# Attention and expert layer on one core: pooled exponentials cross through DRAM in 6 transfers a pair instead of 12, with all orders written anew

## The chip, the cores and the metric

The kernel runs on one core of a Trainium2 chip. The metric is the time of one execution on the device in microseconds; the median of three runs counts. A core has a matmul engine (PE, with its weight loads, PEld), a vector engine (DVE), a scalar engine (ACT), GpSimd (POOL) and SyncE (SP), which here only issues DMAs. Each engine works off its own list of instructions in order and waits on semaphores for the others.

## The reference

```python
B, H, S, D = 8, 8, 576, 64; factor = 4; Sd = 144
q_d, k_d, v_d = (mean of q, k, v over groups of 4 positions)      # (B, H, 144, 64)
out_d = softmax(q_d @ k_d.T / 8) @ v_d                            # pooled attention
out_up = np.repeat(out_d, 4, axis=2)
mask = np.abs(pos[:, None] - pos[None, :]) < 4
out_local = softmax(where(mask, q @ k.T / 8, -1e9)) @ v           # local attention
x = (out_up + out_local) as (B * S, H * D) = (4608, 512)
h = x @ w_in                                                      # (4608, 2048)
P = a0 + a1*h + a2*h**2 + a3*h**3
Q = 1 + |b0|*|h| + |b1|*h**2
out = (P / (Q + 1e-6)) @ w_out                                    # (4608, 512)
```

All of it is float32.

## The kernel before

The attention is done in pairs of heads (`Pair`, `slots`), two pairs at a time; I call two such pairs a quad. A batch has two quads. The expert layer runs over nine blocks of 512 tokens, 16 steps of 128 hidden features each, 144 steps in all: the matmuls of L1084 make h, ACT and DVE turn it into g (L1097 to L1190), and the matmuls of L1214 multiply g by w_out. Both products are split in three terms of a shorter float format, so each step has 12 + 12 matmuls of 128x512. From about 40 us on the attention of later batches is worked in between the steps of earlier ones.

The changed code is that of the pooled attention in batches 3 to 7 (`PT_FROM = 3`), ten quads with 20 "far" pairs. There the exponentials `ep` (queries on partitions, 3 groups of 144 keys) must come to lie with the keys on partitions. For that DVE transposes them in blocks of 32 x 32 (`tp`, L751 and L754), SP writes the blocks to DRAM (`bounce_p<-tp`) and reads them back in another order (`eq<-bounce_p`), all in `moved` (L744). The 144 keys are five blocks of 32, the last of which overlaps its neighbour by 16; only its second half is written. So a pair takes 4 writes of 4 blocks, 4 writes of the half block, 2 big and 2 small reads. `far_pooled_v` (L926) then multiplies `eq` by the pooled values `vq`, 48 keys at a time in 3 steps. The exponentials of the local attention take the same way through `tt`, `bounce` and `eu` (4 writes, 2 reads).

The order of everything is found by a planner (`Plan.run`). Each task has an engine, a cost and, for DMAs, a time to landing; it is due as late as its successors allow, moved by a number from the table `SHIFT`, and at each point the ready task that is due first is taken. The lists of all five engines are then issued in that order. The planner's costs of the transfers are `PT_LOADS` and `DT_LOADS`. SP has at most eight transfers open: the ninth waits for the first (`RING`). Where the plan leaves PE idle in the first 40 us, `warm` puts filler matmuls (L1422).

Of the kernel before, what the change touches and what calls it, by code (L numbers as in the profile page):

```python
# [207 lines left out]
def attention_moe(  # L208
# [117 lines left out]
    bounce_p = nc.dram_tensor("bounce_p", [NPAIR * (B - PT_FROM), SD, 2, 5 * BL], F32, kind="Internal").ap()  # L326
# [222 lines left out]
    def q0(c, i):  # L549
        return min(i * D, SD - D) if far_pooled(c) else i * QC  # L550
# [181 lines left out]
    def turned_blocks(cs, bk, due):  # L732
# [13 lines left out]
        for c in cs:  # L746
            s = c.slot
            if far_pooled(c):

                def turn(s=s):  # L750
                    nc.vector.transpose(  # L751
                        out=s.tp.ap[:, :4], in_=s.ep.ap[:, :, : 4 * BL].rearrange("p i (b x) -> p b i x", x=BL)
                    )
# [5 lines left out]
                for a in range(4):
                    lo, n = a * BL, 2 + a % 2  # L760
                    for i, src, k, m in (
                        (0, s.tp.ap[lo : lo + BL, :4, :n], 0, 4 * BL), (1, s.tp.ap[lo + BL // 2 : lo + BL, 4:, :n], 4 * BL, BL // 2)
                    ):
                        to = far[k : k + m, a // 2, a % 2 * D : a % 2 * D + n * BL]
                        moved(
                            to.rearrange("(b i) x -> i b x", i=min(m, BL)), src.rearrange("p b i x -> p b (i x)"),
                            (s.tp,), (rooms[i][a],), PT_LOADS[i],
                        )
# [9 lines left out]
            if c.far:  # L778
# [7 lines left out]
                for r in range(2):  # L786
# [88 lines left out]
    def weighted(cs, bk, due):  # L875
# [45 lines left out]
        def far_pooled_v():  # L921
            for k in range(NKC):
                for c, x in zip(cs, ava):
                    for j in range(2):
# [803 lines left out]
```

## Time and profile before

| | |
|---|---|
| median of 3 runs | 953.27 us (951.35 to 953.3) |
| the profiled execution | 953.53 us, its span 951.5 us |
| PE busy | 931.4 us (98%) |
| DVE busy | 874.3 us (92%) |
| ACT busy | 775.4 us (81%) |
| mean granted clock of PE | 0.997 |
| reads `eq<-bounce_p` | 40 of 72 KB, 4.4 us to landing (median); 40 of 9 KB, 2.0 us |
| writes `bounce_p<-tp` | 160 of 4 to 48 KB, 1.9 to 2.4 us |
| loads `qk<-in_qk_dram` | 32 of 590 KB, 6.3 us |

The span runs from the first to the last instruction of the program in the profile; the execution's time has 2.0 us more around it. "Busy" of PE counts modelled ends of overlapping matmuls: one of 128x512 is shown with 0.39 us, and the next starts 0.23 us after it.

### The profile page before, as it was taken

How to read it: one execution, taken by the hardware profiler on the slowest of the kernel's cores; microseconds unless marked ns; L12 is line 12 of the kernel's file. 1: busy time of each engine (PE TensorE's matmuls, PEld its weight loads, DVE VectorE, ACT ScalarE, POOL GpSimd, SP SyncE). 2: the span in 40 equal slices, each digit the busy share in tenths (PEclk: the TensorE clock that was granted, in tenths of full speed). 3: DMA queues.
4: the chain of work that ended last, by engine and by line, in shares of the span. 5: the costliest groups of instructions: out<-in, count | busy, mean ns of one | idle time of the engine just before them, and what ended most of it. 6: DMA issues, size and time to landing. Idle time of an engine off the chain costs nothing.

```text
span 951.5 us, 19814 instructions
## 1 busy us (share of the span) xinstructions
PE 931.4 (98%) x7037; PEld 731.9 (77%) x7037; DVE 874.3 (92%) x1567; ACT 775.4 (81%) x1972; POOL 149.2 (16%) x176
## 2 busy tenths in 40 slices
PE   8999999999999999999989999999999999999996
PEld 7756566777787877787878878787878788887885
DVE  6999999999999999999979999999999888988886
ACT  4899999897897979797969798888979676767664
POOL 1032232221203121222213030404020000000000
PEclk9999999999999999999999999999999999999999
DMA  9697855545355556565646565655633010001001
GB/s 296 253 270 211 253 102 96 147 83 146 53 155 118 123 116 139 147 126 116 124 127 114 140 108 164 116 133 107 170 74 82 5 45 1 1 0 45 1 1 44
DMA packets 97578, 108.24 MB, mean 114 GB/s; under 512 B 29480, under 2 KB 79784, under 8 KB 97480
## 3 DMA queue, kind: packets, MB, share of 16 engines
q1 hardware_dynamic: 73960, 85.80, 30.2%
q0 software_dynamic: 23232, 20.66, 16.2%
q8 instruction: 55, 0.90, 0.4%
q10 hardware_dynamic: 288, 0.52, 0.2%
q14 instruction: 43, 0.35, 0.1%
HBM read 85.95 MB, written 20.99 MB: 112 GB/s over the span
## 4 chain that ended last, share of the span: by engine, by line
PE 47%; DVE 26%; ACT 16%; issue 5%; DMA 3%; SPq 2%; DVEq 0%; ACTq 0%
PE psum L1214 19%; PE psum L1084 17%; ACT m L1097 7%; DVE g L1176 6%; PE psum L1072 4%; DVE m L1181 3%; DVE m L1190 3%; DVE m L1141 3%; DVE m L1146 3%; ACT gb L1097 3%; ACT el L624 2%; PE psum L888 2%; DMA eq<-bounce_p 2%; DVE m L1150 2%; SPq L744 1%
## 5 line engine op out<-in xcount | busy, mean ns | idle before, releaser
L1214 PE MATMUL psum<-wh,g 128*128 128x512 f32 x1152 | 373.1, 398 | 3.2 <-DVE g L1176 2.2
L1214 PEld LDWEIGHTS psum<-wh,g 128*128 128x128 f32 x1152 | 214.9, 188 | 58.2 <-DVE g L1176 5.3
L1084 PE MATMUL psum<-xs,wh 128*128 128x512 f32 (+1 forms) x1040 | 258.1, 388 | 0.8 <-ACT gb L1097 0.8
L1097 ACT ACTIVATE m<-psum,cf 128x512 f32<-128x512 f32 x288 | 213.2, 748 | 26.4 <-PE psum L1084 20.3
L1176 DVE TENSOR_TENSOR g<-m,m 128x512 fp32r<-128x512 f32 x288 | 194.3, 685 | 42.7 <-ACT m L1097 36.4
L1084 PEld LDWEIGHTS psum<-xs,wh 128*128 128x128 f32 x1040 | 192.2, 188 | 42.9 <-ACT gb L1097 2.0
L1214 PE MATMUL psum<-wl,g 128*128 128x512 f32 x576 | 224.5, 391 | 0.0
L1097 ACT ACTIVATE gb<-m 128x512 f32<-128x512 f32 x144 | 93.1, 648 | 65.9 <-DVE m L1141 57.8
L1084 PE MATMUL psum<-xs,wl 128*128 128x512 f32 (+1 forms) x520 | 138.2, 388 | 0.0
L1097 ACT ACTIVATE gb<-psum,cf 128x512 f32<-128x512 f32 x144 | 115.4, 802 | 21.2 <-PE psum L1214 20.7
L1214 PEld LDWEIGHTS psum<-wl,g 128*128 128x128 f32 x576 | 108.4, 188 | 21.5
L1084 PEld LDWEIGHTS psum<-xs,wl 128*128 128x128 f32 x520 | 96.3, 188 | 20.0 <-DVE wl L397 0.3
L1141 DVE SCALAR_TENSOR_TENSOR m<-m,cf,m 128x512 f32<-128x512 f32 x144 | 106.9, 742 | 2.1 <-ACT m L1097 1.1
L441 POOL DMA_DIRECT2D vq<-in_vq_dram x60 | 52.2, 918 | 321.7 <-DMA vq<-in_vq_dram 230.0
L1097 ACT ACTIVATE m<-gb 128x512 f32<-128x512 f32 x144 | 92.7, 647 | 11.6 <-DVE m L1146 9.9
L1181 DVE SCALAR_TENSOR_TENSOR m<-m,g 128x512 f32<-128x512 f32 x144 | 98.8, 686 | 2.3
L441 POOL DMA_DIRECT2D pq<-in_qkp_dram x84 | 73.6, 923 | 170.7 <-DMA pq<-in_qkp_dram 106.9
L1190 DVE TENSOR_TENSOR m<-m,m 128x512 f32<-128x512 f32 x144 | 98.5, 684 | 1.6
L1146 DVE TENSOR_TENSOR m<-m,m 128x512 f32<-128x512 f32 x144 | 98.4, 684 | 1.7 <-ACT m L1097 1.7
L1150 DVE TENSOR_TENSOR m<-m,gb 128x512 f32<-128x512 f32 x144 | 98.2, 682 | 1.8 <-ACT gb L1097 0.4
L1097 ACT ACTIVATE m<-psum 128x512 f32<-128x512 f32 x144 | 87.3, 608 | 0.3
L624 ACT ACTIVATE el<-el,nm 128x64 f32<-128x64 f32 x240 | 80.8, 355 | 1.7 <-DVE nm L616 1.7
(101 smaller groups left out, 903.2 us busy)
## 6 DMA issues: line engine op xcount, KB each, us to landing
qk<-in_qk_dram SPq DMA_DIRECT2D x32, 590.0 KB, 6.3
pq<-in_qkp_dram POOLq DMA_DIRECT2D x84, 144.0 KB, 3.5
vw<-in_vw_dram SPq DMA_DIRECT2D x32, 320.0 KB, 11.5
out_dram<-xf SPq DMA_DIRECT2D x34, 256.0 KB, 2.5
bounce<-tt SPq DMA_DIRECT2D x96, 80.0 KB, 1.9
eu<-bounce SPq DMA_DIRECT2D x40, 160.0 KB, 3.3
sl<-in_w_out_dram SPq DMA_DIRECT2D x12, 512.0 KB, 4.8
vq<-in_vq_dram POOLq DMA_DIRECT2D x60, 96.0 KB, 3.4
```

Of the source, the lines that this page charges most:

```text
L441: lambda d=dst, x=src, r=r: nc.gpsimd.dma_start(out=d.ap, in_=rows(x, r), accum_op=ALU.add),
L624: nc.scalar.activation(out=s.el.ap[:, k, j, :], in_=view[:, j, k, :], func=AF.Exp, bias=nm[:, 5 * j + k : 5 * j + k + 1], scale=scale, acc ...
L1072: nc.tensor.matmul(ph.ap, lhsT=bits[0][fc].ap[:, c, :].bitcast(F32), rhs=x.ap[:, c, :], start=(c == 0), stop=(c == NCC - 1),)
L1084: nc.tensor.matmul(ph.ap[:, f * t : (f + 1) * t], lhsT=(high, low)[j][0][fc].ap[:, c, :], rhs=blk.x[i].ap[:, c, t0 : t0 + t], start=(part_ ...
L1097: add("ACT", cost, lambda: nc.scalar.activation(out=out_.ap, in_=in_, func=func, **kw), (room_in, cf, *more), (out_,))
L1141: lambda: v.scalar_tensor_tensor(out=tb.ap, in0=tq.ap, scalar=b1, in1=tb.ap, op0=ALU.mult, op1=ALU.add),
L1146: add("DVE", 0.602, lambda: v.tensor_tensor(out=ta.ap, in0=ta.ap, in1=tq.ap, op=ALU.mult), (ta, tq), (ta,))
L1150: add("DVE", 0.602, lambda: v.tensor_tensor(out=ta.ap, in0=ta.ap, in1=u.ap, op=ALU.add), (ta, u), (ta,))
L1176: return v.tensor_tensor(out=out, in0=x, in1=y, op=ALU.mult)
L1181: lambda: v.scalar_tensor_tensor(out=tb.ap, in0=tb.ap, scalar=CONE, in1=gh.ap.bitcast(F32), op0=ALU.add, op1=ALU.mult),
L1190: add("DVE", 0.602, lambda: v.tensor_tensor(out=ta.ap, in0=ta.ap, in1=tb.ap, op=op), (ta, tb), (ta,))
L1214: nc.tensor.matmul(ob[sub].ap, lhsT=g[i].ap[:, g0 : g0 + P], rhs=flat((high, low)[j][1][fc].ap), start=(fc == 0 and m == 0), stop=(fc == N ...
```

## The change

Five blocks of 32 keys are taken at a stride of 28 (`KB = 28, NKB = 5`: keys 0 to 31, 28 to 59, ..., 112 to 143), so 160 rows hold the 144 keys, some twice. One DVE transpose makes all five. A pair then takes 4 writes, each of all five blocks, and 2 reads of 64 rows x 3 steps x 144 queries. The matmul contracts over 64 rows instead of 48; the values `vq` have zero rows where a key comes for a second time. The planner's costs of the reads and of the local reads are set anew, and the whole table `SHIFT` is replaced, with which all lists change their order. (Lines after the first are one further down, so L744 is now L745 and L926 is L927.)

```diff
-    bounce_p = nc.dram_tensor("bounce_p", [NPAIR * (B - PT_FROM), SD, 2, 5 * BL], F32, kind="Internal").ap()
+    bounce_p = nc.dram_tensor("bounce_p", [NPAIR * (B - PT_FROM), NKB * BL, 2, SD], F32, kind="Internal").ap()
...
     def q0(c, i):
-        return min(i * D, SD - D) if far_pooled(c) else i * QC
+        return (0, D, SD - QC)[i] if far_pooled(c) else i * QC
...
-                def turn(s=s):
-                    nc.vector.transpose(
-                        out=s.tp.ap[:, :4], in_=s.ep.ap[:, :, : 4 * BL].rearrange("p i (b x) -> p b i x", x=BL)
+                flat_ep = s.ep.ap.rearrange("p i k -> p (i k)")
+                src = bass.AP(
+                    tensor=flat_ep.tensor, offset=flat_ep.offset,
+                    ap=[flat_ep.ap[0], [KB, NKB], [SD, NQ], [1, BL]],
+                )
+                add(
+                    "DVE", 0.57, lambda s=s, src=src: nc.vector.transpose(out=s.tp.ap, in_=src), (s.ep,), (s.tp,)
+                )
+                far = bounce_p[c.p - PT_FROM * NPAIR]
+                rooms = [Room(None, [("E", c.p, a)]) for a in range(4)]
+                for a in range(4):
+                    lo, n = a * BL, D + a % 2 * (SD - 2 * D)
+                    to = far[:, a // 2, a % 2 * D : a % 2 * D + n]
+                    moved(
+                        to.rearrange("(b i) x -> i b x", i=BL), s.tp.ap[lo : lo + BL].rearrange("p b i x -> p b (i x)")[:, :, :n],
+                        (s.tp,), (rooms[a],), PT_LOADS[0],
                     )
-                    nc.vector.transpose(out=s.tp.ap[:, 4], in_=s.ep.ap[:, :, SD - BL :])
-
-                add("DVE", 0.62, turn, (s.ep,), (s.tp,))
...
                 for r in range(2):
-                    own = s.eq.ap[r * D : r * D + KQ]
-                    from_ = [rooms[i][a] for i in range(2) for a in (2 * r, 2 * r + 1)]
-                    moved(own[:, :, : 2 * D], back[r][:, :, : 2 * D], from_, (c.halves[r],), PT_LOADS[2], 0.78)
-                    moved(own[:, :, 2 * D :], back[r][:, :, 2 * D + BL // 2 :], from_[1::2], (c.halves[2 + r],), PT_LOADS[1], 0.78)
+                    row = far[0, r]
+                    back = bass.AP(
+                        tensor=row.tensor, offset=row.offset, ap=[[2 * SD, D], [KQ * 2 * SD, NKC], [1, SD]]
+                    )
+                    moved(
+                        s.eq.ap[r * D : (r + 1) * D], back, rooms[2 * r : 2 * r + 2], (c.halves[r],), PT_LOADS[1], 0.6,
+                    )
...
-                            lhsT=c.vp.ap[m : m + KQ, k, :], rhs=c.slot.eq.ap[m : m + KQ, k, :],
+                            lhsT=c.vp.ap[m : m + D, k, :], rhs=c.slot.eq.ap[m : m + D, k, :],
...
-DT_LOADS = (0.25, 0.8)
+DT_LOADS = (0.25, 1.8)
...
-PT_LOADS = (0.15, 0.1, 0.15)
+PT_LOADS = (0.2, 0.7)
...
 SHIFT = {
-    "alone.0": {0: 4.2, 1: -3.7, 2: -24.3, 3: 193.8},
+    "alone.0": {0: -49.2, 1: -66.5, 2: -2.4, 3: 72.7, 4: -11.7},
...
+    rows = [[KB * (r // BL) + r % BL for r in range(k * KQ, k * KQ + D)] for k in range(NKC)]
     vq = np.zeros((B - PT_FROM, NPAIR, 2, D, NKC, POOL, D), v.dtype)
-    vq[:, :, :, :KQ] = v[PT_FROM:].reshape(B - PT_FROM, NPAIR, 2, NKC, KQ, POOL, D).transpose(0, 1, 2, 4, 3, 5, 6)
+    keys, seen = v.reshape(B, NPAIR, 2, SD, POOL, D), set()
+    for k in range(NKC):
+        for r, key in enumerate(rows[k]):
+            if key not in seen:
+                vq[:, :, :, r, k] = keys[PT_FROM:, :, :, key]
+                seen.add(key)
```

The far quads are numbered 0 to 9 in the order in which PE uses them. On SP, at the end of the second pair of quad 4, before: `tp0` and `eq0` are that pair's pooled exponentials, `eu0` its local ones, `out_0_dram` is an output store, `qk0` the load of q and k for a later pair.

```order
L744 DMA bounce_p<-tp0_201 16x96
L1247 DMA out_0_dram<-xf0_0_154 128x512 x2
L744 DMA bounce_p<-tp0_201 32x4x96
L744 DMA eu0_198<-bounce 64x2x320
L744 DMA bounce_p<-tp0_201 16x96
L744 DMA eu0_198<-bounce 64x2x320
L1247 DMA out_0_dram<-xf0_0_154 128x512
L744 DMA eq0_200<-bounce_p 48x3x16 x2
L423 DMA qk0_191<-in_qk_dram 128x1180
L744 DMA eq0_200<-bounce_p 48x3x128 x2
```

The same place now, from the pair's first write on.

```order
L745 DMA bounce_p<-tp0_201 32x5x80 x2
L745 DMA bounce_p<-tp0_201 32x5x64
L745 DMA bounce<-tt0_193 32x4x160
L1248 DMA out_0_dram<-xf0_0_154 128x512 x2
L745 DMA bounce<-tt0_193 32x4x160
L745 DMA eq0_200<-bounce_p 64x3x144
L1248 DMA out_0_dram<-xf0_0_154 128x512 x2
L745 DMA bounce_p<-tp0_201 32x5x64
L745 DMA eu0_198<-bounce 64x2x320 x2
L745 DMA eq0_200<-bounce_p 64x3x144
L424 DMA qk0_191<-in_qk_dram 128x1180
```

The load `qk0`, which stood ahead of the two big reads, now stands behind the last read.

On SP, at the end of the second pair of quad 3, before:

```order
L744 DMA eq0_200<-bounce_p 48x3x16
L744 DMA bounce_p<-tp0_201 32x4x96
L744 DMA eu0_198<-bounce 64x2x320
L744 DMA bounce_p<-tp0_201 16x64
L744 DMA bounce_p<-tp0_201 16x96
L744 DMA bounce_p<-tp0_201 16x64
L744 DMA eu0_198<-bounce 64x2x320
L744 DMA eq0_200<-bounce_p 48x3x128
L744 DMA eq0_200<-bounce_p 48x3x16
L744 DMA eq0_200<-bounce_p 48x3x128
L423 DMA qk0_191<-in_qk_dram 128x1180
```

And now, where `eu1` and `qk1` belong to the other pair of the quad's slots:

```order
L745 DMA bounce<-tt0_193 32x4x160 x2
L745 DMA eu1_209<-bounce 64x2x320
L745 DMA bounce<-tt0_193 32x4x160
L424 DMA qk1_202<-in_qk_dram 128x1180
L745 DMA bounce<-tt0_193 32x4x160
L745 DMA bounce_p<-tp0_201 32x5x64
L745 DMA bounce_p<-tp0_201 32x5x80 x2
L745 DMA eu0_198<-bounce 64x2x320 x2
L424 DMA qk0_191<-in_qk_dram 128x1180
L745 DMA eq0_200<-bounce_p 64x3x144 x2
```

Here the load `qk0`, which stood behind the reads, now stands ahead of both.

On DVE, around the second pair's transposes in quad 4, before:

```order
L1150 TENSOR_TENSOR m1_162<-m1_162,gb1_172 128x512
L689 TENSOR_TENSOR el0_196<-el0_196,sm0_185 128x640
L751 STREAM_TRANSPOSE tp0_201<-ep0_199 128x384
L754 STREAM_TRANSPOSE tp0_201<-ep0_199 128x96
L776 STREAM_TRANSPOSE tt0_193<-el0_196 128x640
L1176 TENSOR_TENSOR g1_168<-m1_162,m5_166 128x512
```

And now:

```order
L690 TENSOR_TENSOR el0_196<-el0_196,sm0_185 128x640
L1151 TENSOR_TENSOR m1_162<-m1_162,gb1_172 128x512
L777 STREAM_TRANSPOSE tt0_193<-el0_196 128x640
L757 STREAM_TRANSPOSE tp0_201<-ep0_199 128x480
L1177 TENSOR_TENSOR g1_168<-m1_162,m5_166 128x512
L1182 SCALAR_TENSOR_TENSOR m3_164<-m3_164,g1_168 128x512
```

The local transpose `tt0` has changed places with the pooled one.

## Rows read from the trace of the kernel before

**Rows 1.** Page: span, then busy us (share of the span) and instructions
```profile
span 951.5 us, 19814 instructions
...
PE 931.4 (98%) x7037; PEld 731.9 (77%) x7037; DVE 874.3 (92%) x1567; ACT 775.4 (81%) x1972; POOL 149.2 (16%) x176
```

**Rows 2.** Busy us (xinstructions) of PE, PEld, DVE, ACT, POOL by stage; clock; DMA
```profile
48.00:168.00 120.00, 117.94 (x892) 75.02 (x891) 119.61 (x230) 118.72 (x340) 37.22 (x42) 1.00 0.73 187
168.00:744.00 576.00, 569.35 (x4555) 458.43 (x4554) 544.56 (x996) 483.47 (x1292) 109.50 (x126) 1.00 0.54 120
744.00:920.00 176.00, 175.04 (x799) 143.87 (x798) 150.47 (x233) 124.93 (x204) 0.00 (x0) 1.00 0.03 13
```

**Rows 3.** Who waited for whom on PE: us in total, times, longest
```profile
PE psum L926 <- DMA eq<-bounce_p: 5.4, 4, 2.9
```

**Rows 4.** Timeline of PE, quad 4: start, us, instruction [idle before]
```profile
491.09 1.54 PE L926 MATMUL psum<-eq,vq 48*64 48x144 f32 x22 [2.88 <-DMA eq<-bounce_p]
...
494.08 0.79 PE L1214 MATMUL psum<-wh,g 128*128 128x512 f32 x1
...
495.38 0.39 PE L1214 MATMUL psum<-wl,g 128*128 128x512 f32 x1
```

**Rows 5.** The clock beside it: stretch, length, PE busy, granted clock, DMA, GB/s
```profile
491.79:495.20 3.41, 3.41 (x69) 0.50 0.21 58
```

**Rows 6.** Timeline of PE, quad 2
```profile
389.00 1.22 PE L926 MATMUL psum<-eq,vq 48*64 48x144 f32 x22 [0.33 <-DMA eq<-bounce_p]
...
390.97 0.50 PE L1214 MATMUL psum<-wh,g 128*128 128x512 f32 x1
...
391.78 0.39 PE L1214 MATMUL psum<-wl,g 128*128 128x512 f32 x1
```

**Rows 7.** Timeline of DVE, second pair of quad 4
```profile
473.43 0.23 DVE L754 STREAM_TRANSPOSE tp<-ep 128x96 f32<-128x96 f32 x1
```

**Rows 8.** Timeline of the DMA queue of SP, quad 4: issue start, us
```profile
473.54 0.78 SPq L744 DMA_DIRECT2D bounce_p<-tp  x2
...
484.65 0.43 SPq L423 DMA_DIRECT2D qk<-in_qk_dram  x1
...
485.12 0.90 SPq L744 DMA_DIRECT2D eq<-bounce_p  x2
```

**Rows 9.** Timeline of DVE, second pair of quad 3
```profile
424.78 0.23 DVE L754 STREAM_TRANSPOSE tp<-ep 128x96 f32<-128x96 f32 x1
```

**Rows 10.** Timeline of the DMA queue of SP, quad 3
```profile
433.84 1.27 SPq L744 DMA_DIRECT2D eq<-bounce_p  x3
435.16 0.44 SPq L423 DMA_DIRECT2D qk<-in_qk_dram  x1
```

**Rows 11.** Timeline of PE, quad 3
```profile
435.49 1.07 PE L1084 MATMUL psum<-xs,wh 128*128 128x512 f32 x4
436.49 1.32 PE L926 MATMUL psum<-eq,vq 48*64 48x144 f32 x22
```

**Rows 12.** Timeline of DVE, second pair of quad 9
```profile
726.56 0.23 DVE L754 STREAM_TRANSPOSE tp<-ep 128x96 f32<-128x96 f32 x1
```

**Rows 13.** Timeline of PE, quad 9
```profile
738.63 1.41 PE L926 MATMUL psum<-eq,vq 48*64 48x144 f32 x22 [0.69 <-DMA eq<-bounce_p]
```

**Rows 14.** Groups of PE by form: busy us, mean ns | idle before
```profile
L560 PE MATMUL psum<-pq 64*64 64x144 f32 x384 | 17.5, 291 | 0.2 <-DVE el L597 0.2
...
L926 PE MATMUL psum<-eq,vq 48*64 48x144 f32 x240 | 12.9, 299 | 5.4 <-DMA eq<-bounce_p 5.4
```

**Rows 15.** Groups of DVE by form: busy us, mean ns | idle before
```profile
L776 DVE STREAM_TRANSPOSE tt<-el 128x640 f32<-128x640 f32 x24 | 19.9, 830 | 0.0
...
L751 DVE STREAM_TRANSPOSE tp<-ep 128x384 f32<-128x384 f32 x20 | 11.2, 558 | 0.0
...
L754 DVE STREAM_TRANSPOSE tp<-ep 128x96 f32<-128x96 f32 x20 | 4.7, 235 | 0.0
```

More of the change, by code (lines that the diff above doesn't have):

```diff
@@ L29 @@
 NKC, KQ = 3, SD // 3
+KB, NKB = 28, 5
 QR = D + QC
@@ L410, in __init__ @@
             self.vp = (vqs if self.far else vps)[p % 2]
-            self.halves = [Room(None, [("Q", p, i)]) for i in range(6)]
+            self.halves = [Room(None, [("Q", p, i)]) for i in range(4)]
         def pos(self, j):
@@ L748, in turned_blocks @@
             if far_pooled(c):
-                def turn(s=s):
-                    nc.vector.transpose(
-                        out=s.tp.ap[:, :4], in_=s.ep.ap[:, :, : 4 * BL].rearrange("p i (b x) -> p b i x", x=BL)
-                    )
-                    nc.vector.transpose(out=s.tp.ap[:, 4], in_=s.ep.ap[:, :, SD - BL :])
-                add("DVE", 0.62, turn, (s.ep,), (s.tp,))
-                far = bounce_p[c.p - PT_FROM * NPAIR]
-                rooms = [[Room(None, [("E", c.p, a, i)]) for a in range(4)] for i in range(2)]
@@ L759, in turned_blocks @@
[L759 to L768, printed above, removed]
@@ L793, in turned_blocks @@
                     own = s.eu.ap[r * D : (r + 1) * D].rearrange("p (g a) k q -> p g (a k q)", g=2)
-                    moved(own, back, rooms[0] + rooms[1], (c.halves[4 + r],), DT_LOADS[1] / 2, 0.8)
+                    moved(own, back, rooms[0] + rooms[1], (c.halves[2 + r],), DT_LOADS[1] / 2, 0.6)
                 continue
@@ L1528 @@
+    "h.1": {0: -20.3, 2: 19.8, 3: -7.8},
+    "h.2": {0: 24.7, 1: 18, 3: 11.1},
+    "h.3": {0: -13.5, 1: 75.8, 2: 143.6, 3: 129.8},
+    "h.4": {0: 358.8, 1: 33, 2: -21.5, 3: 40.2},
+    "h.5": {0: 15.4, 1: 60.8, 2: 233.8},
+    "h.6": {0: 178.7, 2: 1.1},
+    "h.7": {0: 29.1, 2: 24.2},
     "load": {
-        0: -109.3, 1: -1.8, 2: 1.2, 4: 24.9, 5: -47.2, 6: 18.7, 7: -38.8, 8: 9, 9: -30.9, 10: 1.4,
-        11: -16.5, 12: 23.6, 13: 18.5,
+        0: 39.4, 1: 25.5, 3: -62.4, 4: -7.5, 5: -95.3, 6: 77.7, 7: -169.5, 8: 49.5, 9: 10.3, 10: -2.1,
+        12: -0.1, 13: 20.6,
@@ L1553 @@
-    "middle.1": {
-        0: 99.4, 1: -3.9, 2: -21.5, 3: 15.2, 4: 8.1, 6: 2.6, 7: 41.1, 8: -12.7, 9: 7.8, 10: -2.9, 12: 9.2,
+        1: 19.8, 2: -14.2, 4: 347, 5: 16.7, 6: 1.5, 7: 1, 8: -805, 9: -68.6, 10: 5.3, 11: 5.2, 12: 2.9,
+    },
+    "middle.1": {0: -6.6, 2: 1.8, 4: -113.9, 5: 87.2, 6: -62, 7: -15.5, 8: 29.4, 11: 0.2, 12: 91.1},
+    "middle.2": {
+        0: -1.7, 1: 1.9, 2: 126.7, 3: 24.9, 4: -16.3, 5: 1.2, 6: 0.9, 7: 3.2, 8: -136.2, 9: -42.8, 10: -0.7,
+        11: -5.5, 12: -46.4,
@@ L1555 @@
     },
-    "middle.2": {0: -33.4, 1: 103.1, 2: 1, 3: -34.9, 4: 1.4, 6: -26.9, 7: 35.1, 10: 5.5, 11: -66.8, 12: 3.2},
     "middle.3": {
-        0: 4.2, 1: -0.3, 2: -48.3, 3: 24.7, 4: -267.5, 5: 143, 6: -60.1, 7: 54.8, 8: -19.5, 9: 26.4,
-        10: 15.8, 11: -137.6,
+        1: -14.6, 2: -120, 3: 18.6, 4: -337.1, 5: -13.8, 6: -16.5, 7: 8.3, 8: -1.7, 9: 65.6, 10: 162.4,
+        11: -163.4, 12: -72.8,
     },
     "middle.4": {
-        0: 31, 1: -114.7, 2: -5.9, 3: 141.5, 4: -105.5, 5: 36.2, 6: 51.9, 7: 187.8, 8: 145.5, 9: -8.3,
-        10: -23.1, 11: 10.3, 12: -0.2,
+        1: -5.7, 2: -26.8, 3: 16.4, 4: -216.8, 5: 36.7, 6: 69.6, 8: -10.4, 9: 22.4, 10: -38.8, 11: -0.4,
@@ L1627 @@
-    "scores.0": {0: 97.5, 1: 5.8, 2: 3.2, 3: 119.5, 4: -10.9, 5: -54.1, 6: 76.1, 7: 8.2, 8: -0.5},
-    "scores.1": {0: 58.2, 1: -20.6, 2: 1.1, 3: 48.5, 4: 44, 5: -2.7, 6: 34.3, 7: 58.1, 8: 20.3},
-    "setup": {0: -53.4, 1: 13.4, 2: -22.5, 3: 99.9, 4: -14.3},
[6 rows of a table removed]
[8 rows of a table added]
+    },
+    "scores.0": {0: 15.3, 1: 38.6, 2: -54.4, 5: -40.5, 6: 52.5, 7: 144.7, 8: 105.7},
+    "scores.1": {0: 10.1, 1: 15.7, 2: -37.5, 4: 50.7, 5: -14.2, 6: 5.7, 8: 99.8},
+    "setup": {0: 43, 1: -13.5, 2: -21.9, 4: 16.4},
[6 rows of a table added]
     "turned.0": {
[4 rows of a table removed]
[3 rows of a table added]
@@ L1641 @@
     },
     "turned.1": {
[4 rows of a table removed]
-    },
[10 rows of a table removed]
+        0: -13.9, 1: -10.5, 2: 97.5, 3: -32.6, 5: 132.1, 6: 164.7, 7: 87.4, 8: 81.1, 9: 17.8, 11: -50.8,
+        12: 14.4, 13: -0.4, 14: -0.2, 15: -6.2, 17: -10.6, 18: 3.2, 19: -3.6, 20: 67.9, 21: 341.5, 22: 17.4,
+        23: 77.6, 25: 2.2, 26: -21.5,
+    },
[10 rows of a table added]
 }
```

45 lines of the change are left out of this document (18 added, 27 removed), and 147 rows, old and new, of the table SHIFT.

## The prediction

> **What bounds the kernel now.** I read the page's busy times first. PE is busy for 931.4 of 951.5 us, so the whole kernel can lose at most some 20 us without less matmul work [rows 1]. The table by stage says where that idle time lies. From 48 to 168 us PE, DVE and ACT are all over 98% busy; from 168 to 744 us PE is idle for 576.0 - 569.35 = 6.65 us; from 744 to 920 us for 0.96 us [rows 2]. The middle stage is the one in which the changed code runs, so I asked next who made PE wait. One entry holds most of it: the pooled value matmuls L926 wait for the reads of the transposed exponentials, eq from bounce_p, 5.4 us in 4 waits, the longest 2.9 us [rows 3].
>
> I count the ten far quads 0 to 9 in the order in which PE uses them. The worst wait is quad 4's, 2.88 us [rows 4]. It costs more than its length. From 491.79 to 495.20 us the granted clock is 0.50, the lower of the two levels (1.2 GHz instead of 2.4) [rows 5]. From the first L926 to the first expert matmul after it quad 4 takes 494.08 - 491.09 = 2.99 us, and the next three matmuls 495.38 - 494.08 = 1.30 us [rows 4]; quad 2, which waits only 0.33 us, takes 390.97 - 389.00 = 1.97 us and 391.78 - 390.97 = 0.81 us at full clock [rows 6]. So the clock costs 1.02 + 0.49 = 1.5 us more.
>
> Why it waits is seen on SP. The second pair's transposes end at 473.43 + 0.23 = 473.66 us [rows 7]; PE is ready at 491.09 - 2.88 = 488.21 us. The lead is 14.5 us and the way through DRAM took 17.4 us. Of that, 12.0 us went into issuing: from the first write at 473.54 to the last read at about 485.57 us stand 22 issues, writes, reads, local blocks and output stores, 0.573 us from one to the next; and the two big reads stand behind a load of the next pair's q and k, so that the last one lands 5.5 us after its issue [rows 8]. In quad 3 that load stands behind the reads [rows 10]: the last of three reads is issued at about 434.7 us and PE starts at 436.49 us with no wait, so it landed within 1.8 us [rows 11]. Its transposes end at 425.01 us [rows 9], a lead of 11.5 us.
>
> **The change part by part.** Matmuls: the same number. The value matmuls contract over 64 rows instead of 48. L560 has 64 rows and the same 144 columns and takes 291 ns, L926 299 ns [rows 14]. Cost 0; between the two lies 8 ns, for 240 of them 1.9 us at most either way if nothing overlapped. PE has five filler matmuls less in the first 40 us (152, not 157); they stand where PE would wait anyhow: 0.
>
> DVE: one transpose of 480 columns replaces 384 and 96. Before: 558 + 235 = 793 ns. The new one lies between 558 (384 columns) and 830 ns (640 columns) [rows 15]; by a straight line 558 + 96/256 x 272 = 660 ns. That is 20 x 0.13 = 2.7 us less DVE work, in a stage in which DVE is busy 544.56 of 576 us and PE 569.35 [rows 2]. It is beside PE's work: I take 0, with a gain of 2.7 as the other end.
>
> SP: 6 transfers a far pair instead of 12, 120 issues less. Since PE only feels the last read of each quad, I work out for three kinds of quads the lead (end of the second transposes to PE being ready) and the need. One matmul costs PE (1.07 - 0.39)/3 = 0.227 us [rows 6, 11].
>
> - Even quads, as quad 4. On PE the use stands 8 matmuls earlier (a group of four L1084 and four L1214 now come behind it), 1.8 us; on DVE the local transpose of 0.8 us now stands ahead of the pooled one. Lead 14.5 - 1.8 - 0.8 = 11.9 us. Need: from first write to last read 14 issues instead of 22, 13 x 0.573 = 7.4 us, and the q and k load is now behind the last read. For the landing the rows give 1.8 us with nothing large ahead and 5.5 us behind such a load; four output stores stand ahead, so I take 3, nearer the first. Need 10.4 us: no wait. At 5.5 us it would be 12.9, a wait of 1.0 in each of five quads.
> - Odd quads, as quad 3. PE uses them 10 matmuls later, 2.3 us; DVE makes the transposes about 0.5 us later against the g's beside them. Lead 13.3 us. But now the q and k load is issued just ahead of both reads. From first write to last read 15 issues, 14 x 0.573 = 8.0 us, and 5.5 us to land: 13.5 us. I take waits of 0.5 us over the four odd quads 1 to 7; the ends are 0 and, with the lead of before, 4 x 2.0 = 8 us.
> - Quad 9, the last. Its lead was 737.94 - 726.79 = 11.1 us [rows 12, 13]. On DVE three operations instead of one now stand from the transposes to the end of the next g, and 23 matmuls instead of 45 on PE from that step's first L1214 to the use: 1.4 us more and 5.0 us less, 7.5 us by that count. Need: four writes, two local reads, two reads, 7 x 0.573 = 4.0, and 1.8 to land, as no bulk load is left: 5.8 us, and up to 2 more if SP is still busy with the local blocks. I take a wait of 0.3; ends 0 and 2.
>
> Sum: -5.4 (waits) - 1.5 (clock) + 0.5 + 0.3 = -6.1 us. The profiled execution took 953.53 us (span 951.5 and 2.0 around it): 947.4. The median of the three timed runs, 953.27, is 0.26 lower; so I expect 947.2 us.
>
> The trace says that a small read behind a large load lands late, 5.5 us instead of 1.8. The Trainium skill, "DMA: Bandwidth & Descriptors", section "Queues, rings and completion order", has the reason: what SP issues goes to its own ring on each DMA engine, and descriptors there are consumed in ring order. By that rule all four odd quads pay the 5.5 us now, which before only the even ones did; the trace agrees as far as quads 3 and 4 go, and the second rival below is this case.
>
> **The rivals.**
>
> *The gain goes elsewhere.* All orders were written anew, not only SP's. From 48 to 168 us three engines have 0.4 to 2.1 us of idle time [rows 2], so a transfer or an exponential that comes 1 us later there is paid in full. In the odd quads the pooled scores now stand some 29 us of PE work ahead of the use instead of 36, so the softmax between them has less room. Against it: in the middle stage only 6.65 - 5.4 = 1.25 us of waits were of another kind, so orders of this sort keep PE fed but for the DMAs. If new waits of 4 to 7 us arise, or the four waits stay because the landing and not the issuing sets them, the time is 951.5 to 954. Chance 0.19.
>
> *The odd quads wait, slower.* The place is the q and k load ahead of the reads in quads 1, 3, 5 and 7. If the last read is issued as late as in quad 3 before, 434.7 - 425.0 = 9.7 us after the transposes, and lands 5.5 us later, the need is 15.2 us. It decides from a lead under about 13.5 us: with 11.5 the wait is 3.7 in each, 14.8 us, and each such wait is longer than the 2.88 us that brought the half clock, 4 x 1.5 = 6 us. The old waits gone (-6.9), that is +13.9 or 967; with the lead at 12.5 about 10.8 of waits and 3 of clock, +7, or 960. For it: the order puts the load there. Against: PE's use is later, and fewer issues stand in front. Chance 0.11.
>
> *More is gained.* DVE's 2.7 us count after all, or the new order also removes waits outside the far quads: 943 to 945. For it: 20 us of idle in all. Against: the middle and late stages have 2.2 us left to give. Chance 0.08.
>
> **How the numbers follow.** The forecast, 945 to 951, has 0.62. A measurement of this kernel can tell about 0.2%, 1.9 us, from no change; faster is then below 951.4. The forecast and the third rival give 0.70 faster; the first rival, nearly all within 1.9 us, 0.19 the same; the second 0.11 slower. The low end of the range is 953.27 - 6.9 - 2.7 = 943.7, no new waits and DVE's gain on the path, rounded to 944.0; the high end 953.4 takes in most of the first rival and leaves out the second.
>
> **What would show it.** Right: the entry of PE's waits for eq falls from 5.4 us to under 1.5; no stretch at the half clock between the start and the tail; 6 transfers a pair, and reads of even quads that land about 3 us after issue; PE's busy time about as before, its idle time some 5 us less. In the odd quads the last read should land 5 us or more after its issue, and PE start within 1 us of it. The DVE transpose should take about 660 ns. Wrong: waits for eq in the odd quads of 2 us and more with half clock behind them (the second rival); idle time of PE between 48 and 168 us over 4 us, or waits for g in the middle stage of more than 2 us (the first); a DVE transpose above 793 ns; L926 (now L927) above 310 ns.

## The result and the profile after: slower by 0.6%

The changed kernel takes 958.1 us (median of 20 runs, 955.38 to 965.64), the kernel before, run beside it, 953.28 us (20 runs, 949.67 to 956.74). The ratio is 1.006, 95% interval 1.0044 to 1.0077 (an estimate over the single runs; the quotient of the medians is 1.005): slower by some 4.8 us, where the prediction had 6.1 us less. The profiled execution took 955.52 us and is one of the fastest of the 20; only this one has a trace.

The page of the kernel after, and its table by stage, columns as in [rows 1, 2]:

```profile
span 953.7 us, 19602 instructions
...
PE 930.8 (98%) x7032; PEld 732.3 (77%) x7032; DVE 870.7 (91%) x1547; ACT 776.6 (81%) x1972; POOL 148.8 (16%) x176
```
```profile
48.00:168.00 120.00, 115.67 (x882) 73.11 (x881) 117.19 (x228) 117.08 (x337) 36.55 (x42) 1.00 0.74 186
168.00:744.00 576.00, 568.78 (x4494) 458.01 (x4493) 542.34 (x974) 481.25 (x1288) 109.73 (x126) 1.00 0.54 121
744.00:920.00 176.00, 174.04 (x853) 143.79 (x852) 149.37 (x235) 127.48 (x208) 0.00 (x0) 0.99 0.06 18
```

PE's idle time grew from 2.06 to 4.33 us in the early stage, from 6.65 to 7.22 in the middle and from 0.96 to 1.96 in the late one. Who made PE wait, and the clock behind the waits (answers to [rows 3, 5]):

```profile
PE psum L927 <- DMA eq<-bounce_p: 8.5, 5, 2.4
PE psum L1073 <- ACT gb L1098: 2.5, 2, 1.9
```
```profile
340.76:344.17 3.41, 3.41 (x73) 3.29 (x71) 1.05 (x2) 0.49 (x4) 0.00 (x0) 0.50 0.13 33
750.36:753.77 3.41, 3.41 (x73) 3.29 (x72) 0.86 (x2) 0.39 (x3) 0.00 (x0) 0.50 0.00 0
```

The waits for `eq` are 8.5 us now, and they have moved: the even quads wait 0.14 us (quad 4, not counted in the 8.5), the odd quads 1, 3, 5 and 7 wait 2.23, 0.65, 2.42 and 1.27 us, quad 9 waits 1.96 us. Behind those of quads 1 and 9 PE ran at the lower clock, 0.50. Quad 5 shows how such a wait comes about. Here are its second pair's transposes on DVE, SP's queue and PE (answers to [rows 8 to 11]):

```profile
525.50 0.67 DVE L757 STREAM_TRANSPOSE tp<-ep 128x480 f32<-128x480 f32 x1
...
531.42 0.43 SPq L424 DMA_DIRECT2D qk<-in_qk_dram  x1
531.90 0.43 SPq L745 DMA_DIRECT2D bounce<-tt  x1
532.38 1.49 SPq L745 DMA_DIRECT2D bounce_p<-tp  x3
536.75 1.23 SPq L745 DMA_DIRECT2D eu<-bounce  x2
538.09 0.53 SPq L424 DMA_DIRECT2D qk<-in_qk_dram  x1
538.71 1.23 SPq L745 DMA_DIRECT2D eq<-bounce_p  x2
...
543.07 1.31 PE L927 MATMUL psum<-eq,vq 64*64 64x144 f32 x22 [2.42 <-DMA eq<-bounce_p]
```

The transposes end at 526.17 us. A q,k load (`qk1`) goes out at 531.42, the pair's last block writes directly behind it, and then SP stands still from 533.87 to 536.75 us: the reads `eu` wait until the local block has landed, and everything behind them in SP's list waits too. Then `qk0` goes out, and only then both reads of `eq`, the last at some 539.4. PE was ready at 543.07 - 2.42 = 540.65 us, a lead of 14.5 us. The way took 16.9 us. What held SP is named in its own waits, first of quad 1 (325 to 336 us), then of quad 5 (526 to 540 us):

```profile
SPq L745 <- DMA qk<-in_qk_dram: 1.0, 1, 1.0
```
```profile
SPq L745 <- DMA bounce<-tt: 2.8, 1, 2.8
```

In quad 1 a pooled write waits for `qk1` itself: with `qk1` eight transfers are open, and the write is the ninth. (The list that the section on the change gives for quad 3 now is that of quads 5 and 7 in the trace. In quads 1 and 3 the order differs in detail, but there too `qk1`, issued at 325.95 and 428.94 us, stands ahead of the second pair's pooled writes, and `qk0` ahead of both reads.)

Quad 9 has no load, but its list is crowded (answers to [rows 12, 13]):

```profile
739.00 0.68 DVE L757 STREAM_TRANSPOSE tp<-ep 128x480 f32<-128x480 f32 x1
...
739.80 1.56 SPq L745 DMA_DIRECT2D bounce<-tt  x3
741.52 1.35 SPq L745 DMA_DIRECT2D eu<-bounce  x2
742.91 0.59 SPq L745 DMA_DIRECT2D bounce<-tt  x1
743.55 1.89 SPq L745 DMA_DIRECT2D bounce_p<-tp  x4
745.54 1.23 SPq L745 DMA_DIRECT2D eu<-bounce  x2
746.93 1.25 SPq L745 DMA_DIRECT2D eq<-bounce_p  x2
...
750.09 1.92 PE L927 MATMUL psum<-eq,vq 64*64 64x144 f32 x21 [1.96 <-DMA eq<-bounce_p]
```

The pooled writes go out 3.9 us after the transposes, behind the local blocks and the other pair's local reads.

### The profile page after: what moved, and what is told of

The parts are those of the page before. It is cut to its first block, busy times and chain, and to the rows that moved or that the text cites. A ratio compares the mean times of both kernels' runs of the same rounds, so it can differ in the third digit from the quotient of the medians.

```text
span 953.7 us, 19602 instructions
## 1 busy us (share of the span) xinstructions
PE 930.8 (98%) x7032; PEld 732.3 (77%) x7032; DVE 870.7 (91%) x1547; ACT 776.6 (81%) x1972; POOL 148.8 (16%) x176
## 4 chain that ended last, share of the span: by engine, by line
PE 44%; DVE 22%; ACT 21%; issue 6%; DMA 5%; SPq 1%; DVEq 0%; ACTq 0%
PE psum L1215 18%; PE psum L1085 15%; ACT m L1098 8%; ACT el L625 6%; DVE g L1177 4%; PE psum L1073 4%; ACT gb L1098 3%; DVE m L1182 3%; DVE m L1142 2%; DMA eq<-bounce_p 2%; DVE m L1191 2%; DVE m L1147 2%; PE psum L889 2%; DVE m L1151 2%; ACT ep L655 1%
## 5 line engine op out<-in xcount | busy, mean ns | idle before, releaser
L1215 PE MATMUL psum<-wh,g 128*128 128x512 f32 x1152 | 383.6, 399 | 0.7 <-DVE g L1177 0.4
L1098 ACT ACTIVATE m<-psum,cf 128x512 f32<-128x512 f32 x288 | 212.0, 744 | 33.9 <-PE psum L1085 13.5
L1098 ACT ACTIVATE gb<-psum,cf 128x512 f32<-128x512 f32 x144 | 114.2, 794 | 17.0 <-PE psum L1215 16.9
```

The source lines that it names most:

```text
L1098: add("ACT", cost, lambda: nc.scalar.activation(out=out_.ap, in_=in_, func=func, **kw), (room_in, cf, *more), (out_,))
L1215: nc.tensor.matmul(ob[sub].ap, lhsT=g[i].ap[:, g0 : g0 + P], rhs=flat((high, low)[j][1][fc].ap), start=(fc == 0 and m == 0), stop=(fc == N ...
```

## The experiments

Theory A: the loss comes from the q,k loads that the new SP order puts ahead of the second pair's writes and reads in the odd quads; the new transfers are a gain. Rivals: the transfers of 64 rows are slow themselves, or the early stage is what costs. All ratios are to the kernel before, run beside each kernel on the same chip; its medians there were between 951.62 and 953.69 us, so runs of different groups are compared by their ratios.

### The loads moved behind the reads

In the changed kernel, tasks get a tag, and the finished list is edited before it is issued; nothing but SP's list changes.

```diff
-    todo = plan.run()
+    todo = moved_loads(plan.run())
...
+def moved_loads(todo):
+    tagged = {}
+    for t in todo:
+        tagged.setdefault(t.tag, []).append(t)
+    for p in range(PT_FROM * NPAIR, B * NPAIR - 2, 2):
+        last = max(tagged["eq", p] + tagged["eq", p + 1], key=todo.index)
+        for i in (0,):
+            load = tagged["qk", p + 2 + i][0]
+            if todo.index(load) < todo.index(last):
+                todo.remove(load)
+                todo.insert(todo.index(last) + 1, load)
+    return todo
```

With `(0,)` it moves `qk0`:

> The changed kernel; only the q,k load of the even pair for the next quad (qk0, 590 KB) is issued behind the two reads of the second pair's pooled exponentials instead of right ahead of them, in the odd far quads 1, 3, 5 and 7 (in the others it is behind them already). Theory A (the loads that the new order puts ahead of the reads make the odd quads wait): the reads are issued 0.6 us earlier and land about 2.5 us behind their issue, as in the even quads, instead of 3.4 to 5.1. The waits of the odd quads (2.23, 0.65, 2.42, 1.27 = 6.6 us in the profiled run) fall to under 1.5 us together, the wait of quad 9 (1.96) stays, and the time is 951 to 953.5 us, level with the kernel before or just under it. Rival B (the transfers of 64 rows in overlapping blocks are slow in themselves): the waits of the odd quads stay within 1 us each of what they were, time 956.5 to 958.5. Rival C (the idle time of the early stage is what costs): the waits go, but the time stays over 956.

With `(0, 1)` both loads:

> The changed kernel with both q,k loads for the next quad (qk0 and qk1, 590 KB each) behind the last read of the quad's pooled exponentials, in far quads 0 to 8. Theory A says that the first of them, which stands ahead of the second pair's writes, also delays these: their landing by about 1.5 to 3 us, for which SP stands waiting before it can issue the reads. Then the need of the odd quads (end of the second pair's pooled transposes to landing) goes from 13.4 to 16.9 us to the 10 to 11.5 of the even quads, their waits are 0, and the time is 950 to 953 us. Against it: qk1 comes some 8 us later, and the scores of the next quad may wait for it; then the odd quads' waits go but PE waits for qk1 instead, 954 us or more. Rival B (slow transfers): the waits stay.

With `(1,)` only `qk1` (run later):

> The changed kernel with only qk1 behind the last read, in far quads 0 to 8; qk0 stays ahead of the two reads of the odd quads. Theory A': without qk1 ahead of the second pair's block writes SP can issue the reads 2.5 to 4 us earlier (6.4 to 9 us behind the transposes, as in the run with both behind), which is more than the 1.5 to 2.5 us that qk0 costs them; the odd quads' waits are under 1 us together and the time is 948 to 950.5 us, so that either load alone would not have made the loss. Rival (qk0 ahead of the reads decides by itself): the odd quads wait 1 to 2 us each, 954 to 957 us.

Measured: `qk0` alone 949.05 us, ratio 0.9953 (0.9933 to 0.9973); both 947.59 us, 0.9949 (0.9932 to 0.9966); `qk1` alone 948.66 us, 0.996 (0.9942 to 0.9978). The waits of PE for `eq` in the three, in this order:

```profile
PE psum L927 <- DMA eq<-bounce_p: 3.4, 4, 1.0
```
```profile
PE psum L927 <- DMA eq<-bounce_p: 3.2, 3, 1.4
```
```profile
PE psum L927 <- DMA eq<-bounce_p: 2.4, 2, 1.7
```

Both rivals that keep the loss fall: some 10 us come back though the transfers and the order of every other engine stay. The first two runs are faster than their expectations had them. To move either load alone is enough to make the loss go, as the third expectation had it; its rival, that `qk0` decides by itself, fell. The two loads act at different places. With `qk1` alone moved, the last reads of the odd quads go out 7.8 to 10.2 us behind the transposes instead of 9.3 to 13.2. With `qk0` alone moved they go out hardly earlier, 9.4 to 12.8 us, but PE has them 2.4 to 3.3 us later instead of 3.4 to 5.1. What is left are short waits in quads 4 to 6 and in quad 9. How far single waits scatter is seen in quad 9, whose list none of these edits touches: 1.96 us in the changed kernel, 1.05, 1.09 and 1.69 us in these three. Quad 5 with both loads behind, DVE, SP and PE:

```profile
522.82 0.67 DVE L757 STREAM_TRANSPOSE tp<-ep 128x480 f32<-128x480 f32 x1
...
527.41 1.07 SPq L745 DMA_DIRECT2D bounce<-tt  x2
528.52 1.41 SPq L745 DMA_DIRECT2D bounce_p<-tp  x3
530.27 1.23 SPq L745 DMA_DIRECT2D eu<-bounce  x2
531.66 1.23 SPq L745 DMA_DIRECT2D eq<-bounce_p  x2
532.93 1.07 SPq L424 DMA_DIRECT2D qk<-in_qk_dram  x2
...
537.90 0.96 PE L927 MATMUL psum<-eq,vq 64*64 64x144 f32 x24
```

SP stands still for 0.34 us in place of 2.88 before `eu`, the last read goes out 8.8 us after the transposes instead of 13.2, and PE comes to the use 14.4 us after them without a wait.

### The converse: the kernel before with its loads moved

The same edit in the kernel before, where `qk0` stands ahead of reads in the even quads:

> The kernel before; only the q,k load qk0 goes behind the last read of the second pair's pooled exponentials in the even far quads 0, 2, 4, 6 and 8 (in the odd ones it is there already). Theory A: the waits that the prediction counted as 5.4 us (mostly quad 4, 2.88, and quad 0, 1.46) come from that load, not from there being 12 transfers; the reads land 2 to 3 us behind their issue instead of 4.1 to 5.5, the waits fall under 1.5 us, the half-clock stretch behind quad 4 goes, and the time is 948 to 950.5 us, with all 12 transfers in place. Rival (the number of transfers bounds these quads): waits and time stay within 1 us of before, 952.5 to 954.

And the opposite one, `qk0` ahead of the last two reads in the odd quads:

```diff
+    for p in range(PT_FROM * NPAIR + 2, B * NPAIR - 2, 4):
+        load, read = tagged["qk", p + 2][0], sorted(tagged["eq", p], key=todo.index)[-2]
+        if todo.index(load) > todo.index(read):
+            todo.remove(load)
+            todo.insert(todo.index(read), load)
```

> The kernel before; only the q,k load qk0 goes ahead of the last two reads of the second pair's pooled exponentials in the odd far quads 1, 3, 5 and 7, as the changed kernel has it. Theory A: these quads, which did not wait, wait now: the two last reads are issued 0.6 us later and land 4 to 5.5 us behind their issue instead of 1.8 to 2.9, at 13 to 15 us for a PE that is ready at 11.2 to 11.6: 1.5 to 3 us a quad, 6 to 12 us in all, and 958 to 966 us. Rival B (a load ahead of the reads costs little, the new transfers cost): under 1 us a quad, 953 to 955 us.

Measured: behind 949.99 us, ratio 0.9966 (0.9949 to 0.9982), waits for `eq` 1.3 us instead of 5.4. Ahead 960.0 us, ratio 1.008 (1.0051 to 1.0109), waits 9.4 us. Quad 3 in the second, SP and PE, to be held against [rows 10, 11]:

```profile
436.14 0.36 SPq L423 DMA_DIRECT2D qk<-in_qk_dram  x1
436.54 0.91 SPq L744 DMA_DIRECT2D eq<-bounce_p  x2
...
441.07 1.28 PE L926 MATMUL psum<-eq,vq 48*64 48x144 f32 x22 [2.58 <-DMA eq<-bounce_p]
```

The last read lands about 4.1 us after its issue at 437.0, where it had 1.8 us at most. So the place of one load makes or removes the waits with the old 12 transfers as well, and 3.7 of the 6.1 us that the prediction credited to halving them (by the medians, 953.69 and 949.99) were to be had without it.

### The new transfers in the old order

Here the plan of before is kept with its costs and table; the small tasks stay in the plan but issue nothing. PE, ACT and POOL run the list of before; DVE has one transpose a pair instead of two.

```diff
+                    add("SP", ISSUE, None, (s.tp,), (rooms[1][a],), load=PT_LOADS[1], wait=BACK)
...
+                    add("SP", 0.78, None, from_[1::2], (c.halves[2 + r],), load=PT_LOADS[1], wait=BACK)
...
-            t.fn()
+            if t.fn:
+                t.fn()
```

> The new transfers alone, in the order of the kernel before: each pair's six new transfers stand at the places of the six large old ones, the six small ones are left out, and PE, ACT and POOL run before's order instruction for instruction (DVE has one transpose fewer a pair). Theory A (the 6 transfers are a gain, the loss came with the new order's q,k loads): the even quads' waits (1.46, 0.33, 2.88) go, since the last read is issued 1.5 to 3 us earlier against the same lead of 14 us; the odd quads, where qk0 stands behind the reads, stay without a wait; 948.5 to 951 us. Rival B (the reads of 64 rows in overlapping blocks land later): the waits of the even quads stay and odd ones come, 953 to 957 us.

With `qk0` put ahead of both reads in the odd quads, by the edit above with the first read in place of the last but one:

> The new transfers in the order of the kernel before, with one thing taken from the new order: the q,k load qk0 goes ahead of both reads in the odd far quads 1, 3, 5 and 7. In this order the second pair's pooled transposes come 12 us behind the first pair's (5.9 to 7.8 us in the new order) and the last read is issued 5.7 us behind them (9.3 to 13.2 in the new order). Theory A', narrowed by the runs so far (the load ahead of the reads costs only where the reads are issued late as well): issued 0.6 us later and landing up to 5.1 us behind the issue they are there at about 11.4 us against a lead of 11.1: under 0.5 us a quad, 948.5 to 951 us. Rival (the load ahead of the reads costs by itself, as with the old transfers, where it cost 6 to 8 us): 1 us or more a quad, 953 us or more.

And with loads and output stores behind the last read of each quad:

> The new transfers in the order of the kernel before, with both q,k loads and the output stores behind the last read of each quad's pooled exponentials. Theory A: against the old transfers with qk0 behind the reads (949.99 us) this shows what halving the transfers is still worth once no load stands in the way: the waits are all under 0.5 us, quad 9's too (0.86 there), 948 to 950 us, which is no more than 2 us. Rival: halving the transfers is what counts, 945 to 947 us. Against the changed kernel with both loads behind (947.59 us) it shows what the searched order of the other engines is worth: nothing by theory A, 1 to 3 us if that order is better.

Measured: 948.73 us, ratio 0.996 (0.9943 to 0.9977); with `qk0` ahead 947.75 us, 0.9951 (0.9934 to 0.9967); all clear 947.76 us, 0.9958 (0.9943 to 0.9972). The last two are a little faster than expected. The group of value matmuls of the first of them (columns as in [rows 14]; the line is L930 in this kernel):

```profile
L930 PE MATMUL psum<-eq,vq 64*64 64x144 f32 x240 | 9.8, 291 | 0.0
```

No wait is left, though `qk0` still stands ahead of the reads of the even quads there. So the new transfers alone, in the old order, bring a gain, and a load ahead of the reads costs them nothing that can be measured. The gain is not on top of that of the moved load: with no load in the way the new transfers (0.9958) and the old ones (0.9966) cannot be told apart, and neither can the old order and the new one with both loads behind (0.9949). Quad 5 of the second run, SP:

```profile
528.90 0.37 SPq L424 DMA_DIRECT2D qk<-in_qk_dram  x1
529.31 1.23 SPq L745 DMA_DIRECT2D eq<-bounce_p  x2
```

The transposes end at 523.27 us there, so the last read goes out 6.7 us behind them and has 4.6 us to land before PE is ready (534.51 us, lead 11.2). In the changed kernel's order the same read goes out 9.3 to 13.2 us behind the transposes. One reason is shown, the load `qk1` ahead of the pair's writes. A second is read from the traces and was not tried alone: DVE makes the second pair's transposes only 5.9 us (quads 5 and 7) or 7.8 us (1 and 3) behind the first pair's, where it was 12.1, so that the two pairs' transfers come at SP together. By these runs a load costs when it meets a list that is late already.

### The queue or the traffic

The prediction put the late landing down to the ring in which SP's descriptors are consumed in order. So `qk0` of the odd quads went to GpSimd's queue, at the same place:

```diff
-        add("SP", ISSUE, lambda: nc.sync.dma_start(out=s.qk.ap, in_=qk[b, i]), (), (s.qk,), load=cost, at=at)
+        add("SP", ISSUE, lambda: (nc.gpsimd if c.p in (16, 20, 24, 28) else nc.sync).dma_start(out=s.qk.ap, in_=qk[b, i]), (), (s.qk,), load=cost, at=at)
```

> The changed kernel; the q,k load qk0 of the odd far quads 1, 3, 5 and 7 keeps its place ahead of the two reads, but GpSimd issues it on its own queue instead of SyncE. If what delays the reads is that they stand behind 590 KB in the same queue: the reads land 2.5 to 3 us behind their issue, the odd quads' waits fall as in the run with that load behind (1.6 us of waits there), 949 to 951.5 us. If it is the traffic of 590 KB on the DMA engines, whatever the queue: the reads still land 3.4 to 5.1 us behind their issue, the waits stay within 1 us each, 954.5 to 958.5 us.

Measured: 955.91 us, ratio 1.0034 (1.0017 to 1.0051), against 0.9953 with the load behind. Waits and, in quad 1, POOL, SP and PE:

```profile
PE psum L927 <- DMA eq<-bounce_p: 9.2, 7, 3.0
```
```profile
335.60 0.56 POOL L424 DMA_DIRECT2D qk<-in_qk_dram  x1 [9.23 <-DVE g L1177]
...
335.78 1.23 SPq L745 DMA_DIRECT2D eq<-bounce_p  x2
...
341.03 1.24 PE L927 MATMUL psum<-eq,vq 64*64 64x144 f32 x17 [1.22 <-DMA eq<-bounce_p]
```

The reads leave SP with no load ahead of them in their queue, and the last one still lands 4.6 us after its issue at some 336.4; over the four odd quads 4.1 to 5.2 us. With the load behind them PE had `eq` 2.4 to 3.3 us after the last issue. So the other queue does not take the delay away: it goes with the 590 KB in flight, whichever queue they are on. What it is that the load and the reads share, the DMA engines or the memory, was not tried apart. The Trainium skill has a rule that fits, "DMA: Bandwidth & Descriptors", section "Rules for kernel authors": transfers issued from two engines are interleaved on the same 16 DMA engines. The trace agrees as far as another issuing engine did not help; the ring order that the prediction cited is not needed for the delay.

### What is left

Three runs tried to go on from the changed kernel. First nothing large between a quad's first and last read, loads or output stores (they go behind the last read in the order in which they stood):

> The changed kernel, in which nothing large stands between the first read of a quad's pooled exponentials and the last: both q,k loads of the next quad and the stores of the output (262 KB each) go behind the last read, in far quads 0 to 9. Theory A: the waits that the run with both loads behind still had (1.45 in quad 4, 0.65 in quad 6, where two to four stores stand ahead of the last read) fall under 0.5, quad 9's 1.08 stays (no store and no load stands there), 945.5 to 947.5 us. Rival: the stores are not in the way of the reads and the waits stay, 947 to 948.5 us; or the later stores hold up the buffers of the expert layer and the time grows, over 949 us.

Measured: 949.18 us, ratio 0.9964 (0.9948 to 0.998). The waits for `eq` fell to 1.1 us, all in quad 9, but `qk1` now came behind the stores and PE waited for that:

```profile
PE psum L481 <- DMA qk<-in_qk_dram: 3.0, 2, 1.7
```

A miss, above the expected 945.5 to 947.5 us: the stall moved. Then the loads ahead of the stores, and in quad 9 the second pair's pooled writes ahead of the first pair's local reads:

```diff
+        todo[first : last + 1] = span + loads + stores
+    for w in tagged["tp", B * NPAIR - 2]:
+        t = next(t for t in todo if t.tag == ("eu", B * NPAIR - 1))
+        if todo.index(t) < todo.index(w):
+            todo.remove(w)
+            todo.insert(todo.index(t), w)
```

> The changed kernel with nothing large between a quad's first and last read of the pooled exponentials, now with the q,k loads ahead of the stores behind them, and in quad 9 the second pair's four pooled writes issued ahead of the first pair's local reads (1.2 us of issues that they stood behind). By theory A' the waits for the reads are under 0.5 us in quads 0 to 8, PE no longer waits for qk1 (1.32 and 1.67 us in quads 4 and 6 of the run that had the stores first), quad 9's 1.06 us falls to under 0.3, and what stays is the early stage's 4 us: 944.5 to 947 us. Rival (these waits are made good later anyway): 947 to 949 us, as the other orders gave.

Measured: 950.62 us, ratio 0.9988 (0.9971 to 1.0005), the worst miss. Quad 9, SP and PE:

```profile
737.59 0.59 SPq L745 DMA_DIRECT2D bounce<-tt  x1
740.56 1.23 SPq L745 DMA_DIRECT2D eu<-bounce  x2
741.90 1.23 SPq L745 DMA_DIRECT2D eq<-bounce_p  x2
...
745.08 1.34 PE L927 MATMUL psum<-eq,vq 64*64 64x144 f32 x12 [3.70 <-DMA eq<-bounce_p]
```

The local write that was put off holds SP for 2.4 us in front of `eu`, and the reads of `eq` stand behind. PE still waited 2.2 us for q and k loads. The last run has both loads behind as before, and in quad 9 local and pooled writes ahead of the first pair's local reads:

> The changed kernel with both q,k loads behind the last read (as in the run that gave 947.59 us), and in quad 9 all four local and all four pooled block writes of the second pair issued ahead of the first pair's local reads. In the run before this one only the pooled writes went ahead; the pair's last local write came later by that, SyncE stood 2.4 us in front of the second pair's local reads for it, and the reads of the pooled exponentials behind them were issued 9.0 to 9.7 us after the transposes instead of 6.5 to 7.1, so that PE waited 3.70 us instead of 1.08. If that is the reason, they are now issued at 5.6 to 6.4 and PE's wait in quad 9 is under 0.5 us: 945.5 to 948 us. If the reads' own landing is slow in quad 9, the wait stays at 1 us or more, 947 to 949 us.

```profile
733.35 2.03 SPq L745 DMA_DIRECT2D bounce<-tt  x4
735.47 2.04 SPq L745 DMA_DIRECT2D bounce_p<-tp  x4
737.56 2.55 SPq L745 DMA_DIRECT2D eu<-bounce  x4
740.22 1.25 SPq L745 DMA_DIRECT2D eq<-bounce_p  x2
...
743.65 1.20 PE L927 MATMUL psum<-eq,vq 64*64 64x144 f32 x22 [1.56 <-DMA eq<-bounce_p]
```

Measured: 948.04 us, ratio 0.9955 (0.9936 to 0.9973), no better than 0.9949 with the loads alone, and the wait is 1.56 us. Neither branch of the expectation gives the reason: SP does not stand still any more, and PE has the last read 2.8 us after its issue, which is not slow, but SP issues without a pause from 733.35 to 741.47 us, 14 issues in 8.1 us, so that the reads go out 6.7 and 7.3 us behind the transposes. Neither swap tried in quad 9 brought its wait, 3.70 and 1.56 us, below the scatter seen above. The best versions, 947.6 to 948.0 us, are not to be told apart; all beat both kernels.

## Why the prediction was wrong

**Where the old waits came from: right in the place, not in the cause.** Of the 4.7 us of waits in quads 0, 2 and 4, 0.14 us are left, and the half-clock stretch behind quad 4 is gone, as forecast. In quad 4 the need was 11.6 us, not 10.4, against a lead of 11.4; in the other even quads it was below the lead and is not seen. That the number of transfers made the old waits is half of it: they needed the 12 transfers and the load ahead of the reads together. Without the load the 12 transfers wait 1.3 us, none of it in these quads; with the load 6 transfers in the old order wait nothing.

**The odd quads: the step that failed.** "From first write to last read 15 issues, 14 x 0.573 = 8.0 us, and 5.5 us to land: 13.5 us. I take waits of 0.5 us over the four odd quads 1 to 7", so the prediction. The terms as measured, in us:

| | prediction | quad 1 | quad 3 | quad 5 | quad 7 |
|---|---|---|---|---|---|
| transposes to first pooled write | 0 | 1.0 | 3.1 | 1.1 | 0.5 |
| transposes to issue of last read | 8.0 | 9.8 | 9.3 | 13.2 | 12.4 |
| landing of last read | 5.5 | 5.1 | 4.1 | 3.7 | 3.4 |
| need | 13.5 | 14.9 | 13.4 | 16.9 | 15.8 |
| lead | 13.3 | 12.7 | 12.7 | 14.5 | 14.5 |

The waits were 6.6 us in place of 0.5. The lead was about right and the landing was taken too long; what failed is the time to the last issue, put down as issues times 0.573 us with nothing for waits of SP itself. In quads 5 and 7 there are 16 issues, and between the pauses they come every 0.57 to 0.61 us, as taken; but SP stands still in front of `eu` for 2.88 and 3.13 us, until a local write issued behind `qk1` has landed. In quads 1 and 3 the pauses are shorter, 1.1 and 1.0 us in front of `eu` and 1.7 and 0.3 us in front of pooled writes, and in quad 3 the first pooled write goes out 3.1 us late, behind the first pair's transfers. The prediction saw `qk0` ahead of the reads, and its own order rows showed `qk1` ahead of the second pair's writes; it gave that load no cost.

**Quad 9: the time before the first write.** The need was 10.4 us where 5.8 to 7.8 was given, the lead 8.4 where 7.5 was: 1.96 us instead of 0.3. From first write to last read 8 issues took 4.1 us, as taken (4.0), and the landing 2.5 us instead of 1.8. The rest is that the first write went out 3.9 us behind the transposes: "up to 2 more if SP is still busy with the local blocks" was the right cause and too small.

**The clock.** One stretch at half clock went and two came, each 3.41 us long, and each costs 0.5 x 3.41 = 1.7 us of matmuls.

**The second rival was the case, in a mild form.** Its place is the one that the runs show, its size was not: the landing is shorter than 5.5 us and most of the waits stay under 2.3 us. The first rival has a part: idle time between 48 and 168 us rose by 2.3 to 4.33 us, over the 4 us that the prediction named as a sign. It does not set the sign: in the run with both loads behind that stage still has 3.77 us of idle time and the ratio is 0.9949.

**Smaller terms.** The DVE transpose was put at 660 ns and takes 653. L927 takes 320 ns in the profile of after, over the bound of 310 that the prediction named, but that is the half clock in quads 1 and 9: in the run with both loads behind, which has no such stretch in those quads, it is 291.

```profile
L757 DVE STREAM_TRANSPOSE tp<-ep 128x480 f32<-128x480 f32 x20 | 13.1, 653 | 0.2 <-ACT ep L672 0.2
...
L927 PE MATMUL psum<-eq,vq 64*64 64x144 f32 x240 | 13.3, 320 | 8.7 <-DMA eq<-bounce_p 8.5
```

**The sum.** The profiled executions differ by 955.52 - 953.53 = +2.0 us, their spans by 2.2. PE's idle time rose by 2.8 us, from 951.5 - 931.4 to 953.7 - 930.8: the waits for `eq` give 8.5 - 5.4 = 3.1, the early stage 2.3; the rest of the middle stage went from 1.25 to 0.65, of the late one from 0.96 to 0, from 920 us on PE is idle for 6.47 us instead of 7.43, and before 48 us for 2.94 instead of 3.05, 2.6 less together. PE's busy time fell by 0.6 us although one more stretch at half clock is in it; for these 2.3 us I have no row. The median is 2.6 us above the profiled execution. For the executions without a trace the mean granted clock of each is on record. An estimate from it, (1 - clock) x time, averaged: 6.3 us in the 20 of the changed kernel, 2.4 to 3.3 us in those of the kernel before beside the experiments, 2.3 us with both loads behind. So some 3 to 4 of the 4.8 us lost, and some 4 of the 10 us that came back, go with the lower clock; that it fell behind waits like those of quads 1 and 9 is likely but was not seen. The waits for `eq`, 8.5 us in the changed kernel and 3.2 us with both loads moved, do not make up the 10 us by themselves.

## What to carry to other kernels

An in-order queue's issue time is not the number of issues times their spacing: count for each read what it waits for, and which large transfer delays that. Ahead of a small transfer on which another engine will wait, look for bulk traffic in flight, on any queue, and compare lead and need for each place apart; a load that costs nothing measurable ahead of six transfers in the old order costs some 1% in the new one. Before halving the small transfers, try moving the one load that stands in their way.

## What was not expected of the hardware

The lower clock does not follow a wait's length alone: waits of 2.23 us (quad 1) and 1.96 us (quad 9) were followed by 3.41 us at clock 0.50, the longer one of 2.42 us in quad 5 was not, nor one of 2.58 us in quad 3 of the kernel before with `qk0` ahead. Stretch, length, PE busy and clock behind quad 5:

```profile
543.10:546.50 3.40, 3.40 (x78) 2.98 (x79) 1.27 (x3) 1.19 (x5) 0.00 (x0) 1.00 0.23 58
```

And a bulk load on GpSimd's queue delays SyncE's reads about as much as on SyncE's own: 4.1 to 5.2 us to land, against 3.4 to 5.1.
